# Row gathers spread over the experts, the first weights asked for earlier, and one copy moved from VectorE to ScalarE in a scan-then-routed-experts kernel

## The chip, the cores and the metric

The kernel runs on one core of a Trainium2 chip. The metric is device time in microseconds of one launch, from inputs in DRAM to the output in DRAM; lower is better.

## The reference

Two blocks follow each other. The first is a gated linear recurrence (4 batches, 8 heads, 768 steps, head size 48); its output, seen as 3072 tokens of 384 numbers, goes to a mixture of 8 experts in which every expert gets exactly 384 tokens.

```python
f = 1.0 / (1.0 + np.exp(-f_logit))
for t in range(S):
    state = f[:, :, t, :, None] * state + np.einsum('bhd,bhe->bhde', k[:, :, t], v[:, :, t])
    y[:, :, t] = np.einsum('bhd,bhde->bhe', q[:, :, t], state)
x = y.transpose(0, 2, 1, 3).reshape(N, D)
order = np.argsort(-(x @ w_gate).flatten())      # best (token, expert) pairs first
# each token goes to the first expert of that order that still has room (N // E tokens each)
for e in range(E):
    mask = assigned == e
    out[mask] = np.maximum(x[mask] @ w1[e], 0.0) @ w2[e]
```

## The kernel before

**Attention.** The recurrence is worked in 24 chunks of 128 steps (6 in each of 4 batches, all heads at once), software-pipelined by a list of stages. The drain writes the last chunk's result in two halves: `taken0` (L335, VectorE) copies one half from PSUM to `y0`, and `added0` (L339) adds the halves later. A chunk's result is turned on TensorE, copied to a tile `x` by ScalarE (`copy_y`, L349), given its router logits by GpSimd (`with_logits`, L370), and stored to a DRAM array `xd`. The last three chunks are stored from ScalarE's queue, the others from SyncE's. The experts later gather their tokens' rows from `xd`.

**Weights.** Expert e's two weight matrices (1536 KB each) are loaded by `load_weights` (L580). With `behind`, a one-column copy into the weight tile is put in front of the load, so that the load on SyncE's queue can't start before the tile that is copied from is ready. For expert 0 this copy is GpSimd's, two of them, and before the change its source is the last chunk's `x`, after the last store (L743). All other loads hang on a ScalarE copy inside the expert before.

**Routing.** A search in several digits on VectorE, with small counting matmuls on TensorE, finds which tokens an expert takes. A first, short search gives the first two blocks of 128 tokens of expert 0. Between its steps stand `idle_turns`, matmuls whose result nobody reads (L957 to L961). Then the lists for the first two blocks of experts 1 to 5 are made at once (L981 to L998), and a long search of seven rounds assigns the tokens that are left over.

**Experts.** `ffn` (L755) makes the work of one expert for n blocks of 128 tokens: turn the rows so that features lie on partitions, 24 steps `up` into `H` (Relu on ScalarE gives `hT`), 8 steps `down` per block into `O`, a ScalarE copy to a tile `o`, and an indirect DMA on GpSimd's queue that scatters the 128 rows to the output. `o` has three buffers. The rows of expert 0 and of expert 1's first blocks are turned on TensorE (`by_matmul`, L762) and copied from PSUM in two pieces; those of the other experts come in four column pieces (`fetch`, L841, four indirect DMAs per block on GpSimd's queue, tile `xe`, seven buffers) and are turned by VectorE (`by_blocks`, L774, four 32x32 block transposes per block).

**The order.** Each engine runs its instructions in the order in which the program emits them. TensorE's expert steps wait in a list `pe_work`; whenever the search emits a small matmul, the helper `PE` (L662) first takes as many steps off the list as an estimated clock allows. A step on the list may also be a GpSimd fetch of cost 0: then the fetch stands in GpSimd's order after whatever was emitted before it. `add` (L821) puts an expert's turns eight list entries ahead of the list's end. Experts 0 to 5 are put on the list before the long search begins; GpSimd's queue holds, in program order, the gathers of rows, six small gathers of logits (`lg`, L1003) for the search, and the scatters.

Before the change the fetches of experts 2, 3 and 4 (24 piece gathers) are emitted together right behind the six logit gathers (L1007), and those of expert 5 from the list, behind expert 2's scatters. All scatters of experts 0 and 1 are emitted after the 24.

Of the kernel before, what the change touches and what calls it, by code (L numbers as in the profile page):

```python
# [25 lines left out]
def kernel(  # L26
# [11 lines left out]
    nc = tc.nc  # L38
# [45 lines left out]
    early = ahead.enter_context(tc.tile_pool(name="early", bufs=1))  # L84
# [316 lines left out]
    def attention(first, last):  # L401
        for step in range(first, last):
            order = stages
            if step < 2:
                order = begun
            elif step > len(chunks):
                order = finale
            elif step == len(chunks):
                order = drain
            for stage, n in order:  # L410
                if stage is None:
                    for go in extras.pop((step, n), ()):
                        go()
                elif 0 <= step - n < len(chunks):
                    stage(chunks[step - n])
# [208 lines left out]
    def digit_of(d, over, choice, n, between=()):  # L624
        base, r = A[1][:, 128:129], counts["r"]
        if d:
            above, r = rt([n, TH], f"above{n}", FP16), Y[d % 2]
            for h in range(2):
                part = slice(n * h // 2, n * (h + 1) // 2)
                stt(above[:, part], last_of(over[:, part], TH), base,  # L630
                    mid_of(steps[d][:], n // 2), ALU.subtract, ALU.is_ge)
            for go in between:
                go()
            for c in range(n):
                nc.tensor.matmul(out=r[0:TH, 0:E], lhsT=above[:, c, :],
                                 rhs=choice[:, c, :], start=(c == 0), stop=(c == n - 1))
        most, filled = rt([1], "most"), rt([1], "filled", FP16)
        reduce(most[0:TH], r[0:TH, 0:E], ALU.max)
        ts(filled[0:TH], most[0:TH], CAP - 0.5, ALU.is_ge)
        nc.tensor.matmul(out=base, lhsT=units[d][0:TH, :], rhs=filled[0:TH],  # L640
                         start=(d == 0), stop=(d == DIGITS - 1), skip_group_check=True)
        return base
# [77 lines left out]
    with tc.manual_schedule(engines=FIXED):  # L720
        for load, n in ((load_f, 0), (load_k, 0), (load_q, 0), (load_f, 1), (load_v, 0), (load_k, 1),
                        (load_q, 1), (load_f, 2), (load_v, 1)):
            load(chunks[n])
        load_gate()
        for z in range(2):
            nc.sync.dma_start(out=mask[HC * z:HC * z + HC, 1], in_=mask[HC - HC * z:C - HC * z, 0])
        attention(-1, ALL)
        digit_of(0, over0[:], choice0, NT)
        digit_of(1, over0[:], choice0, NT, [
            lambda: gated(chunks[-1]), lambda: added0(chunks[-1]),  # L730
            lambda: stt(first_over[:], over0[:], 0.0, choice0[:, :, 0], ALU.max, ALU.mult),
            *turned_and_stored(-3)])
        for go in turned_and_stored(-2):
            go()
        kind = route.tile([128, KC + 1, NT], FP16, name="kind", tag="kind", bufs=1)
        base = A[1][:, 128:129]
        stt(kind[:, KC], first_over[:], base, steps[1][:, 0:1].to_broadcast((128, NT)),
            ALU.subtract, ALU.is_ge)
        total_c, line_c, blk_c = positions(kind[:, KC:KC + 1], 1, NT, None,
                                           notfirst[:, 0], None, first=T[1])  # L740
        for go in turned_and_stored(-1):
            go()
        load_weights(0, early, 0, behind=chunks[-1]["x"][:, 0:1])  # L743
    attn.close()

    beyond = const([1, 1], I32, "beyond")
# [1 line left out]
    def fast():  # L748
# [6 lines left out]
        def ffn(e, first_block, n, ahead=None):  # L755
            w = 128 * n
            xT = work.tile([128, DC, CAP], FP32, name="xeT", tag="xeT")
            hT = work.tile([128, FC, CAP], FP32, name="hT", tag="hT")
            L = {}

            def turn(i):
                def by_matmul():  # L762
                    X = [bank("Xe", "H"), bank("Xe2", "O")]
                    x = rows[e, first_block + i][:, 0:D].rearrange("t (p d) -> t d p", d=DC)
                    for d in range(DC):
                        nc.tensor.transpose(
                            out=X[d > 0][:, 128 * d:128 * d + 128], in_=x[:, d],
                            identity=ident[:])
                    copy = nc.scalar.copy if e or first_block else nc.vector.tensor_copy
                    copy(out=xT[:, 0, 128 * i:128 * i + 128], in_=X[0][:, 0:128])  # L770
                    nc.scalar.copy(out=xT[:, 1:DC, 128 * i:128 * i + 128],
                                   in_=X[1][:, 128:D].rearrange("p (c t) -> p c t", t=128))

                def by_blocks():  # L774
                    x = rows[e, first_block + i][:, 0:D].rearrange(
                        "t (g c d) -> t g d c", g=4, d=DC)
                    for g in range(4):
                        nc.vector.transpose(  # L778
                            out=xT[:, :, 128 * i + 32 * g:128 * i + 32 * g + 32], in_=x[:, g])
                    V(4, 0.25)  # L780

                return (0.65, by_matmul) if e < 2 and first_block < 2 else (0.0, by_blocks)

            def up(ft, d):
                def go():
                    if d == 0:
                        L["H"] = bank("H", "H")
                    nc.tensor.matmul(out=L["H"][:, 0:w],  # L788
                                     lhsT=slots[e][0][:, d, 128 * ft:128 * ft + 128],
                                     rhs=xT[:, d, 0:w], start=(d == 0), stop=(d == DC - 1))  # L790
                    if d == DC - 1:
                        nc.scalar.activation(out=hT[:, ft, 0:w], in_=L["H"][:, 0:w], func=AF.Relu)  # L792
                        if ahead is not None and ft in (1, 6):
                            load_weights(ahead, pools[ahead % NS], ahead % NS, (ft // 6,),
                                         hT[:, ft, 0:1])
                return 0.22 * n, go

            def down(i, ft):
                def go():
                    if ft == 0:  # L800
                        L["O"] = bank("O", "O")
                    nc.tensor.matmul(out=L["O"][:, 0:D], lhsT=hT[:, ft, 128 * i:128 * i + 128],  # L802
                                     rhs=slots[e][1][:, ft, :], start=(ft == 0),
                                     stop=(ft == FC - 1))
                    if ft == FC - 1:
                        o = work.tile([128, D], FP32, name="o", tag="o", bufs=3)
                        nc.scalar.copy(out=o[:], in_=L["O"][:, 0:D])  # L807
                        nc.gpsimd.indirect_dma_start(  # L808
                            out=outs[next(tiles)][:, :],
                            out_offset=bass.IndirectOffsetOnAxis(ap=token(e, first_block + i),  # L810
                                                                 axis=0),
                            in_=o[:], in_offset=None)
                return 0.65, go

            return ([turn(i) for i in range(n)],
                    [up(ft, d) for ft in range(FC) for d in range(DC)]
                    + [down(i, ft) for i in range(n) for ft in range(FC)])
# [128 lines left out]
        with tc.manual_schedule(engines=engines):  # L946
# [11 lines left out]
            digit_of(2, over0[:], choice0, NT, [last_codes])  # L958
            idle_turns(3, A[0])
            digit_of(3, over0[:], choice0, NT)  # L960
            idle_turns(3, A[0])  # L961
            code = rt([NT], "code", FP16)
            stt(code[:], over0[:], base, code0[:], ALU.is_ge, ALU.mult)
            clock.update(pe=1.0, dve=0.0)
            for e in range(NA):
                ahead = e + 1 if e + 1 < NA else None
                if e:
                    add(ffn(e, 0, 2, ahead))
                    if e == 2:
                        for i in range(2):  # L970
                            pe_work.append((0.0, lambda i=i: fetch(NS, i)))
                else:
                    add(ffn(e, 0, 1, ahead))
                    add(ffn(e, 1, 1))
# [27 lines left out]
            for i in range(NL):  # L1002
# [1 line left out]
                    out=lg[:, i, :], out_offset=None,  # L1004
                    in_=xd[:, :].rearrange("n (a e) -> (n a) e", e=E),
                    in_offset=bass.IndirectOffsetOnAxis(ap=at[:, i:i + 1], axis=0))
            for e in range(2, NS):  # L1007
                for i in range(2):
                    fetch(e, i)
            m = bank("m", "r")  # L1010
            nc.tensor.matmul(out=m[:, 0:KC + 1], lhsT=ones16[:], rhs=total[:], start=True,
                             stop=True)
# [542 lines left out]
```

## Time and profile before

Times of the kernel before, in three runs: 434.4, 434.41 and 436.63 us; median 434.41.

| what | value |
|---|---|
| profiled execution, its own time | 436.54 us |
| its span, first to last instruction | 434.7 us |
| TensorE matmul busy | 413.9 us (95%) |
| VectorE / ScalarE / GpSimd busy | 208.6 / 152.7 / 170.4 us |
| mean granted TensorE clock | 0.966 |
| gathers of row pieces (L850), GpSimd | 80 of 949 ns |
| scatters (L808), GpSimd | 24 of 982 ns |
| attention ends, expert work begins | about 140 us, 157 us |

A time in the views below is microseconds from the start of the span. "Idle before, releaser" is how long the engine had nothing to run and what ended that. The granted clock is the share of full speed at which TensorE was allowed to run.

### The profile page before, as it was taken

What the parts mean: (1) busy time and instruction counts of PE and PEld (TensorE: products, weight loads), DVE (VectorE), ACT (ScalarE), POOL (GpSimd) and SP (SyncE); (2) the same over time, 40 slices, a digit from 0 to 9 for tenths busy, and PEclk for the clock granted to TensorE, in tenths of its full rate; (3) what the DMA queues carried; (4) which work ended last, traced back from release to release, by engine and by line L of the source; (5) the groups of instructions that cost most, each with busy time, mean ns of one, the idle gap of its engine ahead of it and who ended that gap; (6) DMA issues with size and microseconds to landing.
All of it is one profiled execution on the core that took longest, in us unless ns stands there. A gap on an engine that the chain in (4) does not pass through costs nothing.

```text
span 434.7 us, 11230 instructions
## 1 busy us (share of the span) xinstructions
PE 413.9 (95%) x4600; PEld 306.5 (71%) x4600; DVE 208.6 (48%) x721; ACT 152.7 (35%) x374; POOL 170.4 (39%) x300
## 2 busy tenths in 40 slices
PE   7899999999999789999699999999999999999993
PEld 3688888888787567886476868686888865555572
DVE  6589888888888725176446675630000122001000
ACT  3678777777773112331111203021222222112120
POOL 4345454444432210777701710177511777031010
PEclk9999999999999559999889999999999999999999
DMA  8798998888961577256263644411599512010010
GB/s 163 150 170 185 206 211 190 183 183 195 211 169 50 170 250 272 56 184 184 81 197 131 215 150 169 160 50 38 192 324 313 193 52 52 24 41 15 18 38 24
DMA packets 119564, 63.65 MB, mean 146 GB/s; under 512 B 103312, under 2 KB 115728, under 8 KB 118352
## 3 DMA queue, kind: packets, MB, share of 16 engines
q1 hardware_dynamic: 114528, 52.45, 45.3%
q0 software_dynamic: 4544, 9.67, 7.6%
q8 instruction: 38, 0.62, 0.6%
q10 hardware_dynamic: 432, 0.74, 0.5%
q14 instruction: 22, 0.18, 0.1%
HBM read 52.15 MB, written 10.62 MB: 144 GB/s over the span
## 4 chain that ended last, share of the span: by engine, by line
PE 61%; issue 17%; POOL 11%; DMA 5%; DVE 4%; ACT 1%; POOLq 0%; DVEq 0%; ACTq 0%
PE H L788 15%; PE O L802 14%; POOL xe L850 8%; PE T L235 5%; PE A L277 4%; DMA xe<-xd,quad 4%; PE L L172 4%; PE Y L307 3%; POOL out_dram L808 2%; PE L L363 2%; PE T L346 2%; PE small L256 2%; PE Y L318 2%; PE small L200 2%; PE T L107 1%
## 5 line engine op out<-in xcount | busy, mean ns | idle before, releaser
L788 PE MATMUL H<-xeT,w 128*128 128x128 f32 (+2 forms) x720 | 138.6, 349 | 4.1 <-ACT hT L792 4.1
L802 PE MATMUL O<-w,hT 128*128 128x384 f32 x384 | 129.9, 490 | 0.0
L788 PEld LDWEIGHTS H<-xeT,w 128*128 128x128 f32 x720 | 110.2, 197 | 25.8 <-ACT hT L792 4.5
L802 PEld LDWEIGHTS O<-w,hT 128*128 128x128 f32 x384 | 71.0, 190 | 43.5 <-issue 0.2
L850 POOL DMA_INDIRECT xe<-xd,quad x80 | 75.9, 949 | 24.6 <-issue 21.3
L808 POOL DMA_INDIRECT out_dram<-o,tok x24 | 23.6, 982 | 124.8 <-ACT o L807 111.3
L792 ACT ACTIVATE hT<-H 128x128 f32<-128x128 f32 (+2 forms) x120 | 40.8, 341 | 88.1 <-PE H L788 86.9
L778 DVE STREAM_TRANSPOSE xeT<-xe 128x96 f32<-128x96 f32 x80 | 19.7, 287 | 94.9 <-DMA xe<-xd,quad 59.7
L807 ACT COPY o<-O 128x384 f32<-128x384 f32 x24 | 11.5, 478 | 126.3 <-PE O L802 113.9
L285 DVE COPY_PREDICATED am<-mask,A 128x512 f32<-128x512 int32 x48 | 34.6, 725 | 0.3 <-PE A L277 0.3
L210 POOL TENSOR_TENSOR gl<-span,spans 128x4 f32<-128x4 f32 x20 | 3.9, 196 | 50.7 <-PE Y L307 26.9
L277 PE MATMUL A<-qT,kT 48*64 48x128 f32 (+1 forms) x768 | 22.3, 251 | 0.1
L172 PE MATMUL L<-g,wcum 128*128 128x384 f32 x48 | 19.7, 491 | 1.0 <-ACT g L168 1.0
L158 POOL COPY w<-v 64x256 f32<-64x256 f32 x48 | 18.9, 394 | 2.5
L307 PE MATMUL Y<-am,v 64*64 64x64 f32 (+1 forms) x368 | 19.8, 243 | 0.0
L277 PEld LDWEIGHTS A<-qT,kT 48*64 48x64 f32 x768 | 18.7, 133 | 1.0 <-DVE am L285 0.3
L307 PE MATMUL Y<-am,w 64*64 64x128 f32 (+1 forms) x368 | 19.2, 243 | 0.0
L177 DVE TENSOR_SCALAR dl<-L 128x384 f32<-128x384 f32 x24 | 13.3, 555 | 11.3 <-PE L L172 11.0
L430 DVE TENSOR_SCALAR full_r<-cnt,there 128x32 f32<-128x32 f32 x24 | 6.0, 251 | 25.5 <-PE cnt L901 25.5
L307 PEld LDWEIGHTS Y<-am,v 64*64 64x64 f32 x368 | 17.9, 134 | 0.0
L235 PE MATMUL T<-ident,qg 128*128 128x128 f32 x96 | 15.9, 286 | 2.0 <-DVE qg L188 2.0
L307 PEld LDWEIGHTS Y<-am,w 64*64 64x64 f32 x368 | 17.3, 134 | 0.0
(258 smaller groups left out, 545.5 us busy)
## 6 DMA issues: line engine op xcount, KB each, us to landing
w<-in_moe_w_dram SPq DMA_DIRECT2D x18, 1536.0 KB, 8.1
xd<-x SPq DMA_DIRECT2D x21, 240.0 KB, 4.3
f<-in_f_logit_dram SPq DMA_DIRECT2D x24, 192.0 KB, 4.3
k<-in_k_dram SPq DMA_DIRECT2D x24, 192.0 KB, 4.5
q<-in_q_dram SPq DMA_DIRECT2D x24, 192.0 KB, 4.2
v<-in_v_dram SPq DMA_DIRECT2D x24, 192.0 KB, 4.6
xe<-xd,quad POOLq DMA_INDIRECT x80, 3.1
xd<-x ACTq DMA_DIRECT2D x3, 240.0 KB, 2.0
```

Of the source, the lines that this page charges most:

```text
L158: nc.gpsimd.tensor_copy(out=w[HC * z:HC * z + HC], in_=G["v"][HC - HC * z:C - HC * z, H // 2:H])
L172: nc.tensor.matmul(out=G["Lv"], lhsT=wcum[:], rhs=g_bufs[G["i"] % NB][:, :, 0:DH], start=True, stop=True)
L235: nc.tensor.transpose(out=t[:, 128 * hp:128 * hp + 128], in_=G[src][:, 2 * hp:2 * hp + 2, :].rearrange("t h d -> t (h d)"), identity=ident[:])
L277: nc.tensor.matmul(out=A[par][to, 128 * hp + first * j:128 * hp + 128], lhsT=G["kT"][rows, hp, HC * j:HC * j + HC], rhs=G["qT"][rows, hp, ...
L285: nc.vector.copy_predicated(am[:, par].rearrange("s (a b) t -> s a b t", b=2), mask[:].unsqueeze(2).to_broadcast((128, 2, 2, 128)), A[par] ...
L307: nc.tensor.matmul(out=G["Y"][r0][DP * r:DP * r + DP, 128 * blk + first:128 * blk + 128], lhsT=v, rhs=G["am"][rows, h % 2, h // 2, first:128],
L778: nc.vector.transpose(out=xT[:, :, 128 * i + 32 * g:128 * i + 32 * g + 32], in_=x[:, g])
L788: nc.tensor.matmul(out=L["H"][:, 0:w], lhsT=slots[e][0][:, d, 128 * ft:128 * ft + 128], rhs=xT[:, d, 0:w], start=(d == 0), stop=(d == DC - 1))
L792: nc.scalar.activation(out=hT[:, ft, 0:w], in_=L["H"][:, 0:w], func=AF.Relu)
L802: nc.tensor.matmul(out=L["O"][:, 0:D], lhsT=hT[:, ft, 128 * i:128 * i + 128], rhs=slots[e][1][:, ft, :], start=(ft == 0), stop=(ft == FC - 1))
L808: nc.gpsimd.indirect_dma_start(out=outs[next(tiles)][:, :], out_offset=bass.IndirectOffsetOnAxis(ap=token(e, first_block + i), axis=0), in ...
L850: nc.gpsimd.indirect_dma_start(out=t[:, PW * g:PW * g + PW], out_offset=None, in_=xd[:, :].rearrange("n (a x) -> (n a) x", x=PW), in_offse ...
```

## The change

Four edits, and what each does:

1. The load of expert 0's weights is emitted right after the attention stages, with the last chunk's `y0` as what it stands behind, instead of at the end behind the last `x`. The two one-column GpSimd copies move ahead of the last three `with_logits` copies in GpSimd's order, and the two loads ahead of the last three stores in time (those are on another queue).
2. In `by_matmul` the first piece of the very first turned block is copied by ScalarE; it was VectorE's. All other blocks had ScalarE already.
3. The last `idle_turns` before the lists are made has one matmul instead of three.
4. The fetches: only expert 2's (8 pieces) stay behind the logit gathers. Those of experts 3, 4 and 5 are list entries behind the steps of experts 1, 2 and 3. In GpSimd's order: fetch 2, four scatters of experts 0 and 1, fetch 3, two scatters of expert 2, fetch 4, two scatters of expert 3, fetch 5, a small copy `nf2` (L1076), two scatters of expert 4.

Since the list holds two more entries when experts 3 and 4's turns are put in, the order on the other engines moves in one place: VectorE's eight transposes for expert 4 come after that search round's `sums_r` copy instead of two digits earlier, and three `down` steps on TensorE come after a counting group instead of before it.

```diff
         attention(-1, ALL)
+        load_weights(0, early, 0, behind=chunks[-1]["y0"][:, 0, 0:1])
         digit_of(0, over0[:], choice0, NT)
...
         for go in turned_and_stored(-1):
             go()
-        load_weights(0, early, 0, behind=chunks[-1]["x"][:, 0:1])
...
-                    copy = nc.scalar.copy if e or first_block else nc.vector.tensor_copy
-                    copy(out=xT[:, 0, 128 * i:128 * i + 128], in_=X[0][:, 0:128])
+                    nc.scalar.copy(out=xT[:, 0, 128 * i:128 * i + 128], in_=X[0][:, 0:128])
...
             digit_of(3, over0[:], choice0, NT)
-            idle_turns(3, A[0])
+            idle_turns(1, A[0])
...
                     add(ffn(e, 0, 2, ahead))
-                    if e == 2:
+                    if e + 2 < NA:
                         for i in range(2):
-                            pe_work.append((0.0, lambda i=i: fetch(NS, i)))
+                            pe_work.append((0.0, lambda e=e, i=i: fetch(e + 2, i)))
...
-            for e in range(2, NS):
-                for i in range(2):
-                    fetch(e, i)
+            for i in range(2):
+                fetch(2, i)
```

## The prediction

> **What bounds the kernel now.** I read the page first: the share of each engine, and the row of granted clock beside TensorE's busy row.
>
> ```profile
> span 434.7 us, 11230 instructions
> PE 413.9 (95%) x4600; PEld 306.5 (71%) x4600; DVE 208.6 (48%) x721; ACT 152.7 (35%) x374; POOL 170.4 (39%) x300
> PE   7899999999999789999699999999999999999993
> PEclk9999999999999559999889999999999999999999
> ```
>
> TensorE is busy everywhere but in two dents: slices 13 to 15 (141 to 163 us, where attention hands over to the experts) and slice 19 (206 to 217 us). In both its clock falls too. From about 220 us to 433 us it has no wait at all, so what is won or lost in the dents moves the end one for one. Next, what TensorE waited for from 154 to 226 us:
>
> ```profile
> PE H L788 <- ACT hT L792: 4.1, 1, 4.1
> PE Xe L766 <- issue: 1.5, 1, 1.5
> ```
>
> The 4.1 us are put down to ScalarE. ScalarE's timeline tells why it was late, and GpSimd's tells why the scatter was:
>
> ```profile
> 202.34 0.48 ACT L807 COPY o<-O 128x384 f32<-128x384 f32 x1 [5.25 <-PE O L802]
> 215.25 0.48 ACT L807 COPY o<-O 128x384 f32<-128x384 f32 x1 [12.43 <-DMA out_dram<-o,tok]
> ```
> ```profile
> 172.60 0.94 POOL L844 DMA_INDIRECT x<-xd,tok  x1 [19.19 <-DVE found L992]
> ...
> 182.59 0.95 POOL L850 DMA_INDIRECT xe<-xd,quad  x1 [0.30 <-issue]
> ...
> 211.30 0.94 POOL L850 DMA_INDIRECT xe<-xd,quad  x1 [0.30 <-issue]
> 212.55 1.01 POOL L808 DMA_INDIRECT out_dram<-o,tok  x1 [0.31 <-issue]
> ```
>
> GpSimd issues 32 gathers from 172.60 to 212.25, one per 1.25 us, 24 of them pieces. The first scatter stands behind them although its tile `o` was there at 174.1 (copied at 173.64). With three `o` buffers the fourth copy waits for that scatter to land, ScalarE's Relus stand behind the copy, and TensorE stands from 211.96 to 216.07. Then the clock, by stretches (length, then the busy time of TensorE, its weight loads, VectorE, ScalarE and GpSimd; the last three numbers are granted clock, DMA share and GB/s):
>
> ```profile
> 156.00:160.00 4.00, 3.07 (x13) 2.64 (x14) 1.51 (x6) 0.65 (x2) 0.00 (x0) 0.50 0.74 261
> 208.00:212.00 4.00, 3.96 (x20) 3.08 (x18) 3.06 (x18) 0.00 (x0) 3.09 (x4) 1.00 0.20 45
> 212.00:216.00 4.00, 0.00 (x0) 0.00 (x0) 0.63 (x2) 0.75 (x3) 3.09 (x4) 0.80 0.33 111
> 216.00:220.00 4.00, 3.93 (x9) 3.20 (x10) 0.00 (x0) 1.15 (x5) 1.09 (x2) 0.50 0.75 194
> ```
>
> After the stall TensorE runs at half clock until 221.2. Last the handover, TensorE's and GpSimd's timelines:
>
> ```profile
> 154.27 1.14 PE L107 MATMUL A<-idle,ones 128*128 128x384 f16 x3
> 156.93 0.89 PE L766 MATMUL Xe<-ident,x 128*128 128x128 f32 x3 [1.52 <-issue]
> ```
> ```profile
> 150.77 1.19 POOL L844 DMA_INDIRECT x<-xd,tok  x1 [2.43 <-DVE above L433]
> ```
>
> The first rows are gathered from 150.77 and used at 156.93, 6.2 us later, while the weights (asked for at 147.77) move 390 to 490 GB/s. Expert 1's gather, with little beside it, took from 172.60 to 176.06: 3.5 us.
>
> **The fetches (edit 4).** Nothing is removed; 16 pieces leave the burst: 16 x 1.25 = 20 us. The first scatter starts at about 192.6 on the old clock (182.59 + 8 x 1.25) instead of 212.55. The fourth `o` copy (TensorE done at 207.7) finds a free buffer, so the 4.1 us stall goes. So does the half clock behind it: ten `up` matmuls took 4.4 us from 216.07 to 220.50, against 0.226 us each once warm, 2.3 us, so 2.2 us lost; the next eight 2.05 against 1.81 us, 0.2. Sum 2.4 us, with the stall 6.5 us.
>
> [...] For the profiled execution the row decides. The runs are another matter: its own time was 436.54, the median is 434.41, 2.1 us less, and that may just be runs that weren't throttled there. I keep both: 4.1 to 6.5 us.
>
> What the fetches are late for now. Each stands behind the scatters of the expert two before, so it starts when those tiles are copied, then 2 scatters or one (1.3 us each), 8 pieces, and the landing: 2.4 / 3.1 / 6.7 us (least, median, most of all 80; most while weights load, as they do here). On VectorE the transposes stand in the search's queue, so lateness there holds the search, then its counting matmuls on TensorE.
> - Expert 3: tile (1,1) done at 207.7, scatter from 208.3, last piece issued at 208.3 + 1.3 + 7 x 1.25 = 218.4, landed 220.8 to 225.1. VectorE transposes at 231.48, less 6.5 of the stall: 225.0. Cover 0 to 4 us, plus 2.5 us that VectorE waits for the next counting matmul (at 235.61).
> - Expert 4: scatter at 237.75, last piece 247.8, landed 250.2 to 254.5. The transposes are moved behind `sums_r`, which ended at 258.2; but the counting group ahead of it now comes three `down` steps (0.69 us each) sooner, so they begin at about 256.1. Cover 1.6 to 6. They take 1.65 us, to 257.8, and the first `up` step comes at 259.4. Cost 0.
> - Expert 5: scatter at 260.36, landed 272.9 to 277.2, needed 277.87, with 2.3 us of VectorE's wait behind it. The `nf2` copy, now behind these pieces, ends at about 272.0; VectorE's scan reads it at 274.14. Cover 2.1 us.
> All covered: 0. If one cover fails, TensorE pays the excess, and up to 2.4 us of clock.
>
> **The earlier weights and fewer idle matmuls (edits 1 and 3).** `y0` is written by VectorE from 138.01 to 138.70. GpSimd's two copies (0.53 and 0.66 us) follow, so SyncE, which has nothing else, asks at about 139.4 and 139.9 instead of from 147.77. 3.1 MB of weights plus 0.74 MB of the last stores at about 390 GB/s are 10 us: done at about 150 to 151. GpSimd's last three logit copies are 1.2 us later at most; the earliest of their stores goes at 142.7 behind the ScalarE copy of 142.17: 0. The first gather starts at 150.77 as before, is alone, and takes 3.5 us: 154.3. TensorE is ready at 154.27 plus one idle matmul, 0.38: 154.65, where three would have ended at 155.4. So the turns start at 154.7 instead of 156.93: 2.2 us, against 1.5 with three idle matmuls.
>
> [...] The row: a store landed 2.0 us after issue with weights just starting, so 149.3, before the token list (149.73) was ready. [...] I take 2.1, near the row; ends 0 (gather still crowded) and 2.3.
>
> [...]
>
> **The ScalarE copy (edit 2).** VectorE took 0.29 us from 157.42; the same copy on ScalarE takes 0.26 (at 166.56), and ScalarE was idle 10.7 us before. Its second copy began at 157.89, after TensorE's third turn. 0, at most 0.1 either way. VectorE, held 2.8 us at this copy, goes on to build `kind` early, but TensorE's steps in between set the order: 0.
>
> **The sum.** Profiled execution: 436.54 - 2.1 - 6.5 = 427.9. Median: with 6.5, 434.41 - 2.1 - 6.5 = 425.8; with 4.1, 428.2. I take the middle, 427.0; the likeliest case's own range is 425 to 429.
>
> **Rivals.**
> - *The weights gain nothing* (14%): the gather remains crowded, as 0.7 us of a late store and queueing together would do. Against: 8 us more lead for 8 us of traffic. 427.0 + 2.1 = 429.1.
> - *One cover fails* (10%): expert 3 or 5's rows land in the slowest 6.7 us beside weights, and TensorE waits some 2 us and falls to half clock, 2.4. 427.0 + 4.4 = 431.4.
> - *Slower* (7%): GpSimd becomes the pace. The fetch of expert e+2 can't start before expert e ends; if a piece costs p instead of 1.25 us, expert 3's rows are late by 8 (p - 1.25) beyond 2.5 to 6.7 us of cover, and so are 4 and 5's. From p of about 1.9 on (5.2 us late against 2.5 to 6.7) three stalls of some 2 us come, each with 2.4 of clock: 13 us, 440; two of them already pass 434.4. For it: VectorE waits 59.2 us for `xe` after 290 us, where TensorE is never held by it. Against: 1.25 us held through 188 to 212 us, with VectorE busy and weights loading.
> - *No change* (3%): the stall only moves to another buffer, 434.4. Against: between scatters 20 us apart no `o` is short.
>
> **Chances.** Likeliest 66%. A measurement can tell about 0.5% (2.2 us) from no change: faster is below 432.2, so 66 + 14 + 9 of the 10 = 89%; same 4%; slower 7%. The range holds the likeliest case, the first rival and part of the second: 424.5 (all gains at their ends) to 431.
>
> **What would show it.** Right: scatters directly behind 8 pieces, at about 190 us; no TensorE wait of 4 us near 210 and full clock from about 160 to the end; the first turn at about 154.7; experts' `w` issue near 139.4; no TensorE wait for `xeT`. Wrong: `H` waiting for VectorE's transposes near 223, 250 or 272 us; the gather landing later than 155.

## The result, and the profile after

The changed kernel took 429.78 us (median of four runs, 428.31 to 430.13), the kernel before beside it on the same chip 435.41 (four runs, 434.40 to 436.63): ratio 0.9863, 95% interval [0.9822, 0.9904], so 5.6 us faster. (Ratios here and below compare the fast runs alone: on a second chip, used further down, most runs of each kernel were over 1.5% above its fastest, so that medians over all runs there don't give the ratio.) The profiled executions are 428.31 us (span 426.5) after and 436.54 (span 434.7) before. The forecast of 427.0 was 2.8 us too low; its range, 424.5 to 431, holds the time, but the likeliest case's own range, 425 to 429, does not: what holds it is the room left for the first rival, in which the weights gain nothing.

The page of the changed kernel, the same rows as before (line numbers behind the edits have moved by one):

```profile
span 426.5 us, 11226 instructions
PE 408.5 (96%) x4598; PEld 303.0 (71%) x4598; DVE 208.3 (49%) x720; ACT 153.4 (36%) x375; POOL 169.8 (40%) x300
PE   7899999999999769999999999999999999999994
PEclk9999999999999859999999999999999999999998
```

The dent in slice 19 is gone, in both rows. The dent of slices 13 to 15, the handover, is still there. The waits of TensorE from 154 to 226 us, where the largest were 4.1 us for `hT` and 1.5 us at `Xe`:

```profile
PE Xe L766 <- DMA x<-xd,tok: 2.6, 1, 2.6
PE A L640 <- DVE filled L430: 0.4, 1, 0.4
```

GpSimd's and ScalarE's timelines show why the first is gone:

```profile
190.20 0.94 POOL L849 DMA_INDIRECT xe<-xd,quad  x1 [0.30 <-issue]
191.45 1.01 POOL L807 DMA_INDIRECT out_dram<-o,tok  x1 [0.31 <-issue]
192.77 0.98 POOL L807 DMA_INDIRECT out_dram<-o,tok  x1 [0.30 <-issue]
...
207.38 0.97 POOL L807 DMA_INDIRECT out_dram<-o,tok  x1 [4.43 <-ACT o L806]
...
217.44 0.95 POOL L849 DMA_INDIRECT xe<-xd,quad  x1 [0.30 <-issue]
```
```profile
206.62 0.48 ACT L806 COPY o<-O 128x384 f32<-128x384 f32 x1 [4.92 <-PE O L801]
```

The first scatter starts at 191.45 instead of 212.55. The fourth `o` copy (206.62) now waits for TensorE's product, as a copy should, and not for a scatter. Piece gathers still cost 1.25 us from one start to the next (0.94 and 0.30). By stretches (length, busy time of TensorE, its weight loads, VectorE, ScalarE and GpSimd, then granted clock, DMA share, GB/s):

```profile
208.00:212.00 4.00, 4.00 (x22) 3.44 (x21) 2.84 (x16) 1.34 (x4) 3.09 (x4) 1.00 0.40 108
212.00:216.00 4.00, 4.00 (x30) 3.40 (x29) 2.15 (x10) 1.15 (x3) 2.97 (x4) 1.00 0.93 384
216.00:220.00 4.00, 4.00 (x27) 2.85 (x26) 3.05 (x14) 0.96 (x3) 1.89 (x2) 1.00 0.58 119
```

TensorE is full at full clock where it stood and then crawled. Now the handover, TensorE's and GpSimd's timelines and the stores of the last three chunks into `xd`:

```profile
154.02 0.50 PE L107 MATMUL A<-idle,ones 128*128 128x384 f16 x1
157.11 0.88 PE L766 MATMUL Xe<-ident,x 128*128 128x128 f32 x3 [2.59 <-DMA x<-xd,tok]
```
```profile
153.47 1.19 POOL L843 DMA_INDIRECT x<-xd,tok  x1 [9.51 <-DVE above L433]
```
```profile
L378 ACTq DMA_DIRECT2D xd<-x x3: 338/339/381, 143.2 to 146.9; - x3
...
DMA to landing us min/median/max: 5.4/5.4/5.5
```

The first turn is at 157.11, where it was at 156.93: nothing won. The first gather starts at 153.47 instead of 150.77, although its token list was ready at 149.49 (`tok`, 149.32 plus 0.17). What it waits for are the stores: the last was issued at 146.91 and landed 5.5 us later, at 152.4. Before, the last was issued at 147.25 and landed 2.0 us later, at 149.3. The row names VectorE, but this gather reads nothing of `above`; the section on the weights alone shows the same distance to the stores in four traces.

The queue lines of two stretches, which give packets, MB and share of the DMA engines, tell how the stores came to be late. The first stretch is of the profile after, from the issue of the first of the three stores (143.18) for 3.67 us; the second is of the profile before, from the same issue (142.72) for 2.28 us:

```profile
q1 hardware_dynamic: 481, 1.27, 94.2%
q8 instruction: 1, 0.02, 1.6%
```
```profile
q10 hardware_dynamic: 144, 0.25, 27.9%
```

q10 is the queue of these stores, q1 that of the weights. Before, all 144 packets of the first store were through; after, none had moved in the longer stretch, and the other two stores stand behind it on one queue.

The gather's own way was shorter, 3.64 us from its start to the turn instead of 6.16, because the weights were through by then, as three stretches of 1 us show (columns as above):

```profile
150.00:151.00 1.00, 1.00 (x26) 0.69 (x24) 0.93 (x5) 0.00 (x0) 0.00 (x0) 0.50 1.02 388
151.00:152.00 1.00, 0.58 (x8) 0.33 (x6) 0.72 (x4) 0.00 (x0) 0.00 (x0) 0.50 0.16 61
153.00:154.00 1.00, 0.58 (x20) 0.52 (x17) 0.30 (x2) 0.00 (x0) 0.53 (x1) 0.50 0.00 0
```

The same work in both profiled executions, by start on TensorE's timeline:

| step | before | after | difference |
|---|---|---|---|
| first turn of expert 0 (`Xe`) | 156.93 | 157.11 | +0.18 |
| matmul into `m` ahead of the stall | 210.37 | 209.25 | -1.12 |
| fourth counting group (`cnt`) behind it | 224.72 | 216.76 | -7.96 |
| end | 434.7 | 426.5 | -8.2 |

The first row is the weights' part: none. Between the first and the second the half clock of the handover ended at about 160.7 instead of 163.2, which makes up the 1.3 us; in the three other traces with the load at `y0` it ended at 161.2 to 163.2, so it isn't owed to the change. Between the second and the third lie the stall and the half clock behind it, 6.84 us. Nothing more is won or lost after.

This pair shows 8.2 us where the medians differ by 5.6. The profiled execution of before is at the upper end of its times (436.54 of 434.40 to 436.63) and that of after its fastest (428.31 of 428.31 to 430.13).

### The profile page after: what moved, and what is told of

The parts are those of the page before. It is cut to its first block, busy times and chain, and to the rows that moved or that the text cites. A ratio compares the mean times of both kernels' runs of the same rounds, so it can differ in the third digit from the quotient of the medians.

```text
span 426.5 us, 11226 instructions
## 1 busy us (share of the span) xinstructions
PE 408.5 (96%) x4598; PEld 303.0 (71%) x4598; DVE 208.3 (49%) x720; ACT 153.4 (36%) x375; POOL 169.8 (40%) x300
## 4 chain that ended last, share of the span: by engine, by line
PE 70%; issue 15%; POOL 6%; DVE 4%; DMA 3%; ACT 1%; POOLq 0%; DVEq 0%
PE H L787 19%; PE O L801 19%; PE T L235 5%; PE A L277 4%; POOL xe L849 4%; PE L L172 4%; PE Y L307 3%; DMA xe<-xd,quad 2%; POOL out_dram L807 2%; PE L L363 2%; PE T L346 2%; PE small L256 2%; PE Y L318 2%; PE small L200 2%; PE T L107 2%
## 5 line engine op out<-in xcount | busy, mean ns | idle before, releaser
L787 PE MATMUL H<-xeT,w 128*128 128x128 f32 (+2 forms) x720 | 134.8, 343 | 0.0
L787 PEld LDWEIGHTS H<-xeT,w 128*128 128x128 f32 x720 | 107.6, 193 | 20.7 <-ACT xeT L769 0.3
L158 POOL COPY w<-v 64x256 f32<-64x256 f32 x48 | 18.9, 395 | 2.5
L329 DVE TENSOR_TENSOR yT<-Y,yT 128x512 f32<-128x512 f32 x23 | 15.7, 683 | 0.4 <-ACT yT L325 0.3
```

Source lines behind the costliest of these rows:

```text
L158: nc.gpsimd.tensor_copy(out=w[HC * z:HC * z + HC], in_=G["v"][HC - HC * z:C - HC * z, H // 2:H])
L787: nc.tensor.matmul(out=L["H"][:, 0:w], lhsT=slots[e][0][:, d, 128 * ft:128 * ft + 128], rhs=xT[:, d, 0:w], start=(d == 0), stop=(d == DC - 1))
```

## The experiments

The theory: edit 4 alone gives the gain, by freeing the `o` buffers earlier; edit 1 is worth nothing, since what the gather wins in empty queues it loses waiting for stores that now lie beside the weights; edits 2 and 3 are worth nothing. The rivals: edit 1 or the shorter idle matmuls contribute; or the gain comes from something else in the moved fetches (the traffic, the order on VectorE), and not from the buffers. Medians below are each against runs of the kernel before on the same chip.

### The changed kernel again

> The changed kernel once more, beside the others on the same chip, as the mark for them. Theory (the whole gain is the fetches; the earlier weights bring nothing, because the last stores of xd land 5.4 us after issue among the weights and hold the first gather): 429 to 430 us, 5.5 to 6.5 us under the kernel before. A second theory (the weights gain 2 us and the fetches only 4) expects the same time here, and so does a third (the weights cost 2 us and the fetches gain 8).

429.40 us (428.21 to 430.45) against 435.46, ratio 0.9865 [0.9841, 0.9889]. The same result, with another profile: first turn 3.72 us behind the gather's start, stores 4.2 to 6.8 us.

### The fetches alone

The kernel before with both hunks of edit 4:

```diff
-                    if e == 2:
+                    if e + 2 < NA:
                         for i in range(2):
-                            pe_work.append((0.0, lambda i=i: fetch(NS, i)))
+                            pe_work.append((0.0, lambda e=e, i=i: fetch(e + 2, i)))
...
-            for e in range(2, NS):
-                for i in range(2):
-                    fetch(e, i)
+            for i in range(2):
+                fetch(2, i)
```

> The kernel before with edit 4 alone. First theory: same as the changed kernel within 0.7 us, 5 to 7 us under before, first turn at about 157 us, no stall of TensorE near 210. Second theory (the weights are worth 2 us): some 2 us over the changed kernel, 431 to 432. Third theory (the earlier weights cost 2 us): some 2 us under it, 427 to 428.

429.59 us against 435.46, ratio 0.9873 [0.9851, 0.9896]: 5.9 us, all that the whole change gives. TensorE's timeline and its waits from 154 to 226 us have the old handover and no stall behind it:

```profile
157.52 0.88 PE L766 MATMUL Xe<-ident,x 128*128 128x128 f32 x3 [2.45 <-issue]
```
```profile
PE Xe L766 <- issue: 2.5, 1, 2.5
```

The gather started at 150.44 and took 7.08 us to the turn, with the weights beside it.

### The weights alone

The kernel before with edit 1:

```diff
         attention(-1, ALL)
+        load_weights(0, early, 0, behind=chunks[-1]["y0"][:, 0, 0:1])
...
-        load_weights(0, early, 0, behind=chunks[-1]["x"][:, 0:1])
```

> The kernel before with edit 1 alone. First theory: within 1 us of before, the stall of 4.1 us near 210 still there, the last three stores landing some 5.4 us after issue, the first gather at about 153.4 us instead of 150.8 but landing sooner after its issue. Second theory: 2 us under before. Third theory: 2 us over before.

435.28 us against 435.46, ratio 1.0003 [0.9983, 1.0023]: no gain that can be told; the interval leaves room for 0.7 us. The stores take 4.3 to 6.4 us to land (the last 4.3), and the gather starts at 152.30, 1.86 us later than with the fetches alone. GpSimd's timeline, the way of the `xd` stores, and TensorE's timeline:

```profile
152.30 1.55 POOL L844 DMA_INDIRECT x<-xd,tok  x1 [9.74 <-DVE above L433]
```
```profile
DMA to landing us min/median/max: 4.3/4.7/6.4
```
```profile
156.28 0.89 PE L766 MATMUL Xe<-ident,x 128*128 128x128 f32 x3 [1.20 <-issue]
...
214.82 3.67 PE L788 MATMUL H<-xeT,w 128*128 128x256 f32 x10 [3.91 <-ACT hT L792]
```

The first turn comes 1.24 us earlier than with the fetches alone. That pair alone doesn't tell, since attention's end and the gather differ from one execution to the next; counted from the start of the copy to `y0` (L337 in the traces) all traces of this chip can be compared:

| trace | weights asked for | `y0` to first turn | gather's start to first turn |
|---|---|---|---|
| before, fetches alone, four `o` buffers | behind the last store | 18.92, 20.51, 19.37 | 6.16, 7.08, 6.13 |
| after, again, weights alone, without 2 and 3 | at `y0` | 18.64, 18.87, 19.22, 18.97 | 3.64, 3.72, 3.98, 3.75 |

Some 2.7 us won by the gather (means 6.5 and 3.8), most of it given back by the stores ahead of it. That it is the stores, four traces show: in the order of the second row the last store landed 5.5, 4.2, 4.3 and 4.9 us after its issue, and the gather started 1.1 us behind that landing in each. In the traces of the first row it started 1.0 us behind the token list instead (150.77 behind 149.73 before), with the stores long landed. Nor is it the weights' own end: with the weights alone both matrices had landed at 149.9, the last store at 151.2. The 0.7 us between the means of the first column are within what the traces of one row differ by, and the times can't tell 0.7 us from nothing.

### Four `o` buffers

The kernel before, nothing moved; one buffer more for `o`, one fewer for `xe` to make room:

```diff
-                        o = work.tile([128, D], FP32, name="o", tag="o", bufs=3)
+                        o = work.tile([128, D], FP32, name="o", tag="o", bufs=4)
...
-            t = rows[e, i] = work.tile([128, D], FP32, name="xe", tag="xe", bufs=7)
+            t = rows[e, i] = work.tile([128, D], FP32, name="xe", tag="xe", bufs=6)
```

It was run twice, first on another chip than the runs so far, the second chip:

> The kernel before with four buffers for o instead of three, paid for with six xe buffers instead of seven; no fetch is moved and every engine keeps its order. If the gain of edit 4 is the stall behind the fourth o copy and the half clock after it, this one has it too: 429 to 430 us, as the fetches alone (429.6), with no wait of TensorE near 210 and the scatters still only behind the 24 pieces at about 212 us. If the gain came from anything else that the new order of fetches does, the time stays at 433 us or more.

There every kernel took some 60 us longer: before 496.0 us (485.7 to 499.4), this one 496.89, ratio 0.999 [0.9868, 1.0111], too wide to tell. Lines of TensorE's and ScalarE's timelines show that something else bounds on that chip:

```profile
183.12 0.91 PE L766 MATMUL Xe<-ident,x 128*128 128x128 f32 x3 [2.15 <-issue]
...
192.21 0.91 PE L766 MATMUL Xe<-ident,x 128*128 128x128 f32 x3 [7.76 <-issue]
```
```profile
182.79 0.28 ACT L792 ACTIVATE hT<-H 128x128 f32<-128x128 f32 x1 [2.58 <-issue]
191.88 0.28 ACT L792 ACTIVATE hT<-H 128x128 f32<-128x128 f32 x1 [8.81 <-remote]
202.37 0.27 ACT L770 COPY xeT<-Xe 128x128 f32<-128x128 f32 x1 [10.22 <-issue]
```

ScalarE stands here for up to 10 us, and the rows give only `remote` or `issue` for what ended that, no engine and no transfer of the program. TensorE's turns stand behind it: those of expert 1's two blocks begin within 0.1 us of the ends of the Relus at 182.79 and 191.88. The first of the turns was done at 184.0, yet its copy began at 202.37. Late rows don't explain it: from 171 to 177.5 us the gathers' queue moved 0.50 MB in 192 packets in this trace, and just as much in the trace on the first chip below, in which ScalarE has no such wait after 140 us. Why ScalarE stood wasn't settled. The set decides nothing between the theories, and was repeated on the first chip:

> [...] If the gain of edit 4 is the stall behind the fourth o copy and the half clock after it: 429 to 430 us, no wait of TensorE near 210, the first scatter still at about 212 us. If the gain came from anything else that the new order of fetches does: 433 us or more.

430.27 us against 435.62, ratio 0.9886 [0.9868, 0.9904]: 5.35 us, nearly the whole gain, without moving one fetch. GpSimd's timeline has the first scatter as late as ever; ScalarE's has the fourth copy running ahead of it; TensorE's clock row has no second dent:

```profile
211.60 1.01 POOL L808 DMA_INDIRECT out_dram<-o,tok  x1 [0.30 <-ACT hT L792]
```
```profile
206.78 0.48 ACT L807 COPY o<-O 128x384 f32<-128x384 f32 x1 [4.92 <-PE O L802]
```
```profile
PEclk9999999999999559999999999999999999999998
```

So the stall was one of buffers, with the scatters' place in the queue as its cause, and a fourth buffer removes it as well as the new order does.

### Without edits 2 and 3

The changed kernel with `idle_turns(3, A[0])` and the choice of engine for the first copy put back:

```diff
-                    nc.scalar.copy(out=xT[:, 0, 128 * i:128 * i + 128], in_=X[0][:, 0:128])
+                    copy = nc.scalar.copy if e or first_block else nc.vector.tensor_copy
+                    copy(out=xT[:, 0, 128 * i:128 * i + 128], in_=X[0][:, 0:128])
...
-            idle_turns(1, A[0])
+            idle_turns(3, A[0])
```

> The changed kernel with VectorE's copy and three idle matmuls put back. Theory: the first gather lands at 156 to 157 us in the changed kernel, after three idle matmuls would have ended (155.4), and the copy costs the same on both engines: within 0.7 us of the changed kernel, 429 to 430.3. Rival: the two edits are worth 0.7 us or more either way (fewer idle matmuls let the clock come later, or VectorE freed early lets the lists come sooner).

On the second chip 490.81 us against 496.0, ratio 0.9847 [0.973, 0.9963], too wide to tell 0.7 us. On the first:

> The changed kernel with VectorE's copy and three idle matmuls put back, on another chip. Theory: within 0.7 us of the changed kernel (429.4), since the first gather lands after three idle matmuls would have ended. Rival: worth 0.7 us or more either way.

429.60 us against 435.62, ratio 0.9865 [0.9847, 0.9883], beside 0.9865 for the changed kernel: the two edits together bring nothing that can be told, as predicted. They weren't tried apart. TensorE still waits 1.6 us for the rows at that place with three idle matmuls, so taking two of them away only makes a wait longer.

### The weights ahead of the stores

If the stores lose by lying beside the weights, the weights have to be asked for when no store runs. Here they go 10 us earlier still, at the last full attention step (about 129.5 us), and are through (at 141.9) before the last three stores are issued:

```diff
-        load_weights(0, early, 0, behind=chunks[-1]["y0"][:, 0, 0:1])
+    later(LAST, lambda: load_weights(0, early, 0))
```

> The changed kernel with expert 0's weights asked for at about 129 us, after the last q, k and v loads, with nothing they stand behind, so that they have landed before the last three stores are issued. First theory: those stores land in 2.0 us again, the first gather starts at about 150.8 and lands at 154.3, the first turn is at about 154.7 us, and the time is 2 us under the changed kernel, 427 to 428. Second theory (what holds the gather is not the stores but the token list or the weights' own landing): first turn at about 157, time as the changed kernel's. Third theory (weight traffic in attention's end slows its loads or stores): slower than the changed kernel by 1 us or more.

428.32 us against 435.46, ratio 0.9835 [0.9812, 0.9857]. The same kernel in the two later sets:

> Both matrices asked for at 129 us once more, for a second trace. If the pauses of TensorE at 137 and 143 us belong to the weights beside attention's end they are there again, and the time is 428.3 within 0.5 us; if they were chance they are gone from this trace, the first turn is at about 154.7 us, and the profiled execution is under 427.5.

> Both matrices at about 129 us, on another chip, for a second trace and as the mark for the run with the matrices apart. If TensorE's pauses at 137 and 143 us belong to weights beside attention's end, they are there again and the time is 428.3 within 0.5 us; if they were chance, they are gone and the first turn is at about 154.7 us.

On the second chip 490.93 us; on the first 428.33 against 435.62, ratio 0.9835 [0.9818, 0.9852]. The last three stores land sooner, the gather starts 1.0 us behind its token list, and TensorE goes from its idle matmul into the turns without a wait. But TensorE paused twice at attention's end, inside groups of matmuls, where no other trace of this chip but the next one has a pause. Its timeline, and the stores:

```profile
137.26 0.28 PE L363 MATMUL small<-wg_rows,yT 128*64 128x8 f32 x3 [0.37 <-issue]
...
143.82 0.58 PE L346 MATMUL T<-ident,yT 128*128 128x128 f32 x2 [0.88 <-issue]
...
157.33 0.88 PE L766 MATMUL Xe<-ident,x 128*128 128x128 f32 x3
```
```profile
DMA to landing us min/median/max: 2.0/2.0/2.4
```

The repetition has both pauses again (0.20 and 0.88 us). Their cause isn't shown: the profile names nothing that TensorE waits for. Net, 18.28 us from `y0` to the first turn in both traces, and a median 1.1 us below the changed kernel's in the first set: half of what the first theory expected (427 to 428 us, first turn at 154.7).

### The first matrix ahead of the stores, the second behind the gather

Half the bytes at about 129 us, and the second matrix, which is needed only at the first `down`, behind the first gathered rows:

```diff
-        load_weights(0, early, 0, behind=chunks[-1]["y0"][:, 0, 0:1])
+    later(LAST, lambda: load_weights(0, early, 0, (0,)))
...
                 fetch(0, i)
+            load_weights(0, early, 0, (1,), behind=rows[0, 0][:, 0:1])
```

> The changed kernel with expert 0's first matrix asked for at about 129 us and the second only when the first gathered rows have landed (about 154.5). Theory: no weights move beside the last stores nor beside the first gather, and only half as many beside attention's end as in the run with both at 129 us (428.3), where TensorE paused twice for nothing that the profile shows (0.37 and 0.88 us): 427 to 428 us, first turn at about 154.7. Rival: the second matrix lands later than the first down step needs it (about 164 us), TensorE waits there and the time is 429 or more. Second rival: the pauses are chance, and it is the same as that run, 428.3.

> Expert 0's first matrix at about 129 us, the second behind the first gathered rows, on another chip. Theory: 427 to 428 us, no pause of TensorE at 143 us and one of about 0.3 us at 136 us, first gather landed 3.5 us after its issue. Rival: the second matrix lands later than the first down step needs it, TensorE waits there, 429 or more. Second rival: as with both at 129 us, 428.3.

On the second chip 491.84 us, ratio 0.9958 [0.9838, 1.0078]. On the first 427.80 against 435.62, ratio 0.9832 [0.981, 0.9854], the lowest median of all, about 1.6 us below the changed kernel's 429.40, and not to be told from the version ahead of it. GpSimd's and TensorE's timelines, and the stores:

```profile
151.65 1.20 POOL L843 DMA_INDIRECT x<-xd,tok  x1 [7.31 <-DVE above L433]
```
```profile
137.05 0.29 PE L363 MATMUL small<-wg_rows,yT 128*64 128x8 f32 x3 [0.37 <-issue]
...
155.59 0.89 PE L766 MATMUL Xe<-ident,x 128*128 128x128 f32 x3
```
```profile
DMA to landing us min/median/max: 2.0/2.0/2.0
```

All stores land in 2.0 us, the gather starts 1.04 us behind its token list (150.61), and the first turn comes 16.75 us after `y0`, 2.2 less than the mean of the changed kernel's kind (18.9). The second pause is gone with the second matrix. This is what edit 1 was reckoned to bring to the first turn (154.7 in the working, 16.7 after `y0`), from one trace; of the orders tried only this one, with an early first matrix and a late second one, brings it.

## Why the prediction was right or wrong

**The fetches: right in mechanism and size.** The stall and its half clock were put at 6.5 us for the profiled execution; 6.84 lie between the matmul into `m` and the fourth counting group. For the median 4.1 to 6.5 were kept, and their middle, 5.3, taken; the fetches alone gave 5.9, four buffers 5.35. That it was buffers, and not another effect of the moved gathers, is shown by the four-buffer kernel.

**The covers: all held.** TensorE never waited for `xeT`. Expert 3's last piece was issued at 217.44, 1 us before the 218.4 of the working, and the transposes began at 223.53, where 225.0 was expected, with the rows there:

```profile
223.53 1.63 DVE L777 STREAM_TRANSPOSE xeT<-xe 128x96 f32<-128x96 f32 x8
```

Expert 4's pieces began at 231.08 and expert 5's at 253.81, each some 8 us earlier than costed (239.05 and 261.7 by the scatters of the old profile), as everything was by then. The slower rival asked for pieces of 1.9 us; they stayed at 1.25.

**The weights: the step that failed.** The working said "a store landed 2.0 us after issue with weights just starting, so 149.3, before the token list", and put the gather at 150.77 "as before", a gain of 2.2 us. Measured is no gain: ratio 1.0003 alone, 429.40 against 429.59 with the fetches. The mis-sized term is the landing of the last store: 4.2 to 5.5 us in the four traces with the load at `y0`, not 2.0. The 2.0 came from a trace in which the weights were asked for 0.5 us after the last store; with 3 MB of them asked for ahead of the stores, of which 0.93 MB had moved when the first store was issued (143.18 in the trace of after), that row no longer applied. With 5.4 in its place the store lands at 152.7, the gather starts at 153.7 and the turn is at 157.2; measured are 153.47 and 157.11. The gather's own term was right: 3.5 us predicted, 3.64 measured.

The 0.7 us of a late store with which the first rival reckons is an estimate of the author's that no run shows: in the four traces the last store took 2.2 to 3.5 us more to land than before. In the trace of after the first store moved no packet for 3.67 us while the weights' queue moved 481. The working also looked at the last store alone, where the three stand behind each other. Why the first store's packets waited isn't shown.

The first rival, in which the weights gain nothing, has the result's time (429.1 against 429.4 and 429.8). Of the 2.8 us that 427.0 was too low, 2.1 are the weights; 1.0 is that the kernel before had a median of 435.41 this time and 434.41 in the three runs that the sum started from; 0.3 go the other way.

**The copy and the idle matmuls: right**, 0 within the 0.8 us that the runs can tell.

**The clock: right in kind.** The working had half clock follow the stall in the profiled execution. In both traces with the stall it came, at different length: ten `up` matmuls took 4.64 us in the trace of before and 3.67 in that of the weights alone, against about 2.3 at full clock. In the trace of before the clock fell at about 214.4, 2.4 us after TensorE stopped (211.96). In the trace of the weights alone TensorE stood from 210.91 to 214.82; here are two stretches ahead of the clock's fall, and the one after (columns as above, granted clock third from the end):

```profile
209.00:212.40 3.40, 1.91 (x11) 1.26 (x9) 2.01 (x11) 0.00 (x0) 2.71 (x3) 1.00 0.18 43
212.40:215.80 3.40, 0.98 (x5) 0.88 (x6) 0.00 (x0) 1.52 (x5) 2.56 (x3) 1.00 0.42 158
215.90:219.20 3.30, 3.30 (x15) 2.49 (x14) 0.44 (x3) 0.38 (x1) 0.26 (x1) 0.50 0.91 257
```

There it fell at about 215.8, 4.9 us after TensorE stopped and 1.0 us after it went on. What sets the moment isn't shown. The kernel before varies by 2 to 3 us from run to run; that this loss, which differed by 1 us between the two traces, is all of the spread wasn't tested. The lower end of the range, 424.5, is 1.1 us below what the fetches and the weights give at their ends (434.41 - 6.5 - 2.3 = 425.6), and no run shows that room; what the runs show is a half clock at the handover that ended at 160.7 to 163.2 us in the four traces with the load at `y0`, and at 163.2 before.

## What to carry to other kernels

Read an engine that waits for another back to the buffer that ran short, and count what stands in the queue ahead of the instruction that frees it: here 24 gathers of 1.25 us stood ahead of a scatter, and either a different order or one more buffer was worth the same 5 to 6 us. When a large load is moved forward, list the small transfers that it will newly lie beside, and whether something on the path waits for them; a landing time read off a trace without that load may not hold: 2.0 us became 4.2 to 6.8 here. Then look for a place for the load where nothing on the path is in flight, in pieces if need be; here that lowered the median by another 1.1 to 1.6 us.

## What had not been expected of the hardware

- A 240 KB store on one queue, with 3 MB of weights asked for ahead of it on another, landed after 4.2 to 6.8 us instead of 2.0 in four traces. In the trace of after the first of the stores moved no packet for 3.67 us after its issue (0.9 us in the trace of before).
- In both traces with the stall near 210 us TensorE's clock was halved: 2.4 us after TensorE stopped in the trace of before, where it stood 4.1 us, and 4.9 us after it stopped in that of the weights alone, where it stood 3.9 us and the clock fell 1.0 us after it went on.
- With weights loading beside the end of attention, TensorE paused 0.2 to 0.9 us inside matmul groups, with no releaser in the profile. The longer pause was not there when half of the bytes were moved elsewhere. The cause is open.
- On the second chip ScalarE stood for up to 10 us at a time with no engine or transfer of the program as its releaser, and every kernel run on both took 60 to 67 us longer than on the first (before 496.0 against 435.62, four `o` buffers 496.89 against 430.27). The study's differences could not be told apart there.
